# A mixture-of-experts kernel: the last expert's few-slot products in four pieces instead of one run

## The chip, the cores and the metric

The kernel runs on one core of a Trainium2 chip. The metric is device time in microseconds (us) of the whole program, the median of the runs; lower is better. The core has TensorE (PE, matrix products; PEld is its weight load), VectorE (DVE), ScalarE (ACT), GpSimd (POOL, which issues the gathers here) and SyncE (SP, which issues plain transfers). ACT issues some transfers too.

## The reference

Three layers follow each other. Only the last two matter here:

```
# layer 2: each token goes to one expert e (8 of them), x is 2 x 768 tokens of 512
h = np.maximum(x[b, s] @ w1[e], 0.0)
out[b, s] = p[e] * (h @ w2[e])
# layer 3, on that output x
theta = x @ w_theta
zr, zi = x * np.cos(theta), x * np.sin(theta)
y = np.einsum('ts,bsd->btd', w_tok_r, zr) + np.einsum('ts,bsd->btd', w_tok_i, zi)
u = x + y
result = u + np.maximum(u @ w_ch, 0.0)
```

Layer 1 is a local attention that makes the x of layer 2.

## The kernel before, in words

Tokens are sorted by expert into slots. The eight experts are taken in the order of their loads, each with a fixed capacity of slots (288 down to 144), in tiles of 128. The last expert, with 144, has a full tile and a rest of 16 slots ("few", held 32 wide). Results by slot are written to a buffer in HBM, yd, and layer 3 gathers its rows back in token order, in 12 blocks of 128 tokens (k = 0 to 11).

The few slots of the last expert are handled by a Python generator, `y_few`: it takes a PSUM tile `few`, issues the products of `mm2_few` (L1596: 32 matrix products, eight for each of four pairs of hidden chunks, weights 32 columns wide and 128 columns streamed), then scales the sum on ACT into the tile y0 (L1656, shown in rows as y<-few) and stores it from SP to yd (L1657). Each `next(few)` in layer 3's code issues what stands up to the next `yield`.

Layer 3 works block by block. For block k, in the program's names:

- `gather_y(k)` (L1774) and `gather_q(k)` (L1783, four quarter gathers) bring rows of yd to SBUF, as yg and xq.
- `h_tr(k)` transposes the block: blocks 0 and 1 on PE (L1807, sixteen products with the identity, b<-yg), later ones on DVE (L1798, xTf<-xq).
- `h_xh(k)` (L1814, ACT) and `h_xl(k)` (L1827, DVE) split the result into a high part xh and a low part xl.
- `h_theta(k)` (L1843, PE) makes theta in 12 products: eight with xh, four with xl.
- `trig_a`, `trig_s`, `trig_b`, `trig_c` turn theta into the parts z of x·sin and x·cos, on ACT and DVE (sine at L1871, high parts z at L1904 on ACT, low parts at L1909 on DVE). Blocks 0 and 1 do this in two halves of 256 columns, `lo` and `hi`.
- `h_mix(k, d)` (L1929, PE) multiplies z by the token weights, for a quarter d of the columns, in 12 products. d = 0 and 1 use the half `lo`, d = 2 and 3 the half `hi`.

The text calls these theta(k), mix (k, d), xh(k) and so on. Each engine works through its own list in the order in which the code above issues it (the order is written by hand; no scheduler changes it), and waits by semaphores for other engines' results. `job_load` issues loads of layer-3 weights, here from ACT's queue; `JBUFS` is 3. At the start of layer 3 the order by hand is: theta(0), transposes of block 0, few, transposes of block 1, trig(0) `lo`, mix (0,0), theta(1), trig(0) `hi`, mix (0,1), and on.

Of the kernel before, what the change touches and what calls it, by code (L numbers as in the profile page):

```python
# [104 lines left out]
def by_quad(ap):  # L105

    return ap.rearrange("p (q j c) -> p j q c", q=4, c=32)
# [8 lines left out]
def kernel(  # L116
# [1270 lines left out]
    with ExitStack() as mctx:  # L1387
# [9 lines left out]
        def width(r, i):  # L1397


            M = RCAP[r] - i * 128  # L1400
            return 32 if M <= 32 else 64 if M <= 64 else 128
# [186 lines left out]
        def mm2_few(u, out=None):  # L1588

            r = u // 8  # L1590
            i = RTILES[r] - 1
            c, out = width(r, i), out or yps[r][i]
            for v in (u, u + 1):
                hx, w = fews.pop(v)
                for g in range(128 // c if c < 128 else 0):
                    PE.matmul(  # L1596
                        out[g * c : (g + 1) * c, : 4 * c],
                        lhsT=hx[:, :c],
                        rhs=w.rearrange("p (j q c) -> p q j c", q=4, c=32)[:, g * c // 32 : (g + 1) * c // 32],
                        start=(v % 8 == 0),  # L1600
                        stop=(v % 8 == 7),
                    )
# [15 lines left out]
        def groups_out(n, M, W):  # L1618

            return yd[n : n + M, :].rearrange("m (g c) -> g m c", c=W)  # L1620
# [26 lines left out]
        def y_few():  # L1647

            out = pA_[0].tile([128, 512], F32, tag="a", name="few")
            yield  # L1650
            for u in range(8 * E - 8, 8 * E, 2):
                mm2_few(u, out)
            yield
            W, M = 4 * width(E - 1, 1), width(E - 1, 1)
            yo = y0[:, 384 : 384 + W]
            A.activation(yo, out[:, :W], AF.Copy, scale=pslot.pop(RBASE[E - 1] + 1))  # L1656
            SP.dma_start(groups_out(YLAST + 128, M, W), yo)  # L1657
# [107 lines left out]
    with ExitStack() as hctx:  # L1765
# [24 lines left out]
        def h_tr(k, pool=None):  # L1790
            if k >= NB:
                return
            b, t = divmod(k, NT)
            if t == 0:
                xTb[b] = hb.tile([128, 4, S], F32, tag="xTf", name="xTf")
            if k >= VT:
                xps[k] = xTb[b][:, :, t * 128 : (t + 1) * 128]
                V.transpose(  # L1798
                    xps[k].rearrange("p j (i a) -> p i j a", i=4),
                    xqs.pop(k).rearrange("p (i j c) -> p i j c", i=4, j=4),  # L1800
                )
                return
            tp = (pool or pB).tile([128, 4, 128], F32, tag="a" if pool else "b", name="b")
            for j in range(4):
                for q in range(4):
                    rows = by_quad(x2s[k])[:, j, q]
                    PE.matmul(tp[32 * q : 32 * q + 32, j], lhsT=rows, rhs=ident, start=True, stop=True)  # L1807
            xps[k] = tp
# [26 lines left out]
        def h_theta(k, pool=None):  # L1835
            if k >= NB:
                return
            xh, xl = xparts.pop(k)
            th = ths[k] = (pool or pB).tile([128, DM], F32, tag="a" if pool else "b", name="th")
            prods = ((xh, wth[0]), (xh, wth[1]), (xl, wth[0]))  # L1840
            for n in range(12):
                (xa, wa), j = prods[n // 4], n % 4
                PE.matmul(th, lhsT=xa[:, j], rhs=wa[:, j], start=(n == 0), stop=(n == 11))  # L1843

        def trig_a(k, c=slice(0, DM), tick=lambda: None):

            if k >= NB:
                return
            if k not in trig:
                trig[k] = [hb.tile([128, DM], F32, tag=n, name=n, bufs=2) for n in ("kk", "rr", "si")]  # L1850
            th = (ths[k] if k else ths[k][c.start // 256])[:, c]
            kk, rr, si = [x[:, c] for x in trig[k]]
            A.activation(kk, th, AF.Copy, scale=1.0 / TWO_PI, bias=MAGIC)
            tick()
            if k < VT:
                V.tensor_scalar(kk, kk, MAGIC, None, op0=ALU.subtract)
            else:
                A.activation(kk, kk, AF.Copy, bias=-MAGIC)
            tick()
            V.scalar_tensor_tensor(rr, kk, -C1, th, op0=ALU.mult, op1=ALU.add)  # L1860
            tick()
            V.scalar_tensor_tensor(rr, kk, -C2, rr, op0=ALU.mult, op1=ALU.add)
            tick()
            V.tensor_scalar(rr, rr, 3.1415925, -3.1415925, op0=ALU.min, op1=ALU.max)

        def trig_s(k, c=slice(0, DM)):

            if k >= NB:
                return
            kk, rr, si = trig[k]  # L1870
            A.activation(si[:, c], rr[:, c], AF.Sin)  # L1871
            A.activation(kk[:, c], rr[:, c], AF.Sin, scale=0.5)
            A.activation(kk[:, c], kk[:, c], AF.Square)
            if k >= VT:

                A.activation(kk[:, c], kk[:, c], AF.Copy, scale=-2.0, bias=1.0)
# [17 lines left out]
        def trig_b(k, c=slice(0, DM), eng=V):  # L1894
            trig_i(k, c, eng)
            trig_r(k, c)
# [20 lines left out]
        def h_mix(k, d):  # L1917
            b, t = divmod(k, NT)
            if t == 0 and d == 0:
                big = [pA.tile([128, 512], F32, tag="a", name="a") for _ in range(6)]  # L1920
                acc[b] = [(big[d], big[4 + d // 2][:, (d % 2) * 256 : (d % 2) * 256 + 256]) for d in range(4)]
            z = zs[k]
            n = 0
            for ri in (1, 0):
                c = ri * NT + t
                zh, zl = z[2 * ri], z[2 * ri + 1]
                for za, wa in ((zh, wtok(0, c)), (zh, wtok(1, c)), (zl, wtok(0, c))):
                    for o, lo, hi in ((0, 0, 512), (1, 512, 768)):
                        PE.matmul(  # L1929
                            acc[b][d][o],  # L1930
                            lhsT=za[:, d * 128 : (d + 1) * 128],
                            rhs=wa[:, lo:hi],
                            start=(t == 0 and n == 0 and (o == 0 or d % 2 == 0)),
                            stop=(t == NT - 1 and n == 5 and (o == 0 or d % 2 == 1)),
                        )
                    n += 1
# [56 lines left out]
        xh, xl = [hb.tile([128, 4, 128], F32R, tag=n, name=n) for n in ("xh", "xl")]  # L1993
        pA_.append(pA)
        few = y_few()
        next(few)
        xTb[0] = hb.tile([128, 4, S], F32, tag="xTf", name="xTf")
# [16 lines left out]
        x2s[0] = x.rearrange("p j c -> p (j c)")  # L2014
        next(few)
        h_tr(1)
        lo, hi = halves
        trig_a(0, lo)
        mid = [None, partial(trig_s, 0, lo), None, None, partial(trig_i, 0, lo, V)]
# [13 lines left out]
        trig_l(0, 0, lo)  # L2033
        h_xl(1)
        h_mix(0, 0)
        next(few, None)
        for _ in range(JBUFS):
            job_load()
        jstate["eng"] = SP
        h_theta(1)  # L2040
        trig_s(0, hi)
        trig_b(0, hi, V)
        trig_c(0, hi, V)
# [133 lines left out]
```

## Time and profile before

| | |
|---|---|
| median of 3 runs | 467.25 us (466.7 to 468.66) |
| the profiled execution, its own time | 466.93 us |
| its span, first to last instruction | 465.0 us |
| PE busy | 457.9 us, 98% of the span |
| DVE, ACT, POOL busy | 344.0, 262.3, 142.9 us |
| mean granted clock of PE | 0.999 |

The profiled execution is one run; its span is what the trace shows, and 1.9 us of its time lie around it. Times in rows are us from the span's start; layer 3 begins near 288 us. Busy shares are means over stages with different limits; which engine bounds a stage is read from who waits for whom there. A row of a timeline merges like instructions that follow each other.

### The profile page before, as it was taken

To read this page: it belongs to the slowest core of one execution; us is meant where nothing else is said; L and a number is where in the kernel's file an instruction comes from. 1 tells how busy PE (TensorE), PEld (TensorE's weight loads), DVE (VectorE), ACT (ScalarE), POOL (GpSimd) and SP (SyncE) were. 2 spreads that over 40 slices of the span, in tenths; PEclk is the share of its full clock that TensorE was granted. 3 is DMA by queue.
4 is the path that set the end of the run, shared out by engine and by line. 5 is a ranking of instruction groups with operands and counts; after the bars stand their busy time and mean duration, and the time that the engine had idled before them with its cause. 6 is when DMAs were issued, how large, how long until landed. Compare 5 with 4: busy or idle time off the path is not lost.

```text
span 465.0 us, 9578 instructions
## 1 busy us (share of the span) xinstructions
PE 457.9 (98%) x3346; PEld 378.7 (81%) x3346; DVE 344.0 (74%) x946; ACT 262.3 (56%) x623; POOL 142.9 (31%) x203
## 2 busy tenths in 40 slices
PE   8999999999999999999999999999999999999996
PEld 4677777788888898888787788888888888888886
DVE  5888889768687697887888776687997897741522
ACT  5988786822456666655755544556765665630300
POOL 8602313204032404040514302654874441000400
PEclk9999999999999999999999999999999999999999
DMA  8978577715957788788999993521253110000022
GB/s 241 367 231 248 184 240 253 252 47 158 356 167 225 265 296 270 257 277 270 318 348 307 305 312 132 165 91 48 79 152 109 43 49 24 0 35 34 28 87 93
DMA packets 61770, 85.60 MB, mean 184 GB/s; under 512 B 6248, under 2 KB 40296, under 8 KB 61720
## 3 DMA queue, kind: packets, MB, share of 16 engines
q1 hardware_dynamic: 52212, 62.06, 40.8%
q0 software_dynamic: 5552, 12.55, 8.8%
q10 hardware_dynamic: 3956, 10.36, 6.6%
q8 instruction: 27, 0.44, 0.4%
q14 instruction: 23, 0.19, 0.1%
HBM read 73.56 MB, written 11.38 MB: 183 GB/s over the span
## 4 chain that ended last, share of the span: by engine, by line
PE 90%; ACT 4%; DVE 3%; issue 1%; DMA 1%; POOL 0%; DVEq 0%
PE a L1929 22%; PE o L1580 15%; PE h L1524 10%; PE h L1505 8%; PE b L1966 7%; PE th L1843 7%; PE s L574 4%; PE x L653 3%; PE o L1596 3%; PE pt L629 3%; ACT pr L606 2%; PE tr L1341 1%; PE y L670 1%; DVE sm L596 1%; ACT ps L638 1%; PE h L783 1%
## 5 line engine op out<-in xcount | busy, mean ns | idle before, releaser
L1929 PE MATMUL a<-wtokr,z 128*128 128x512 f32 x480 | 85.3, 336 | 0.0
L1929 PEld LDWEIGHTS a<-wtokr,z 128*128 128x128 f32 x480 | 74.2, 188 | 10.0
L1580 PE MATMUL o<-w2s,hh 128*128 128x512 f32 x192 | 62.7, 406 | 0.0
L606 ACT ACTIVATE pr<-sm,st 128x256 f32<-128x256 f32 (+1 forms) x96 | 46.0, 483 | 15.3 <-DVE st L596 15.2
L1524 PE MATMUL h<-xT,w1s 128*128 128x288 f32 (+3 forms) x384 | 51.4, 284 | 0.5 <-DVE xT L1347 0.5
L1524 PEld LDWEIGHTS h<-xT,w1s 128*128 128x128 f32 x384 | 48.7, 189 | 3.4 <-issue 0.6
L1783 POOL DMA_INDIRECT xq<-yd,Lall x40 | 42.4, 1059 | 25.2 <-issue 9.8
L1487 DVE TENSOR_TENSOR w2s<-raw,w2s 128x512 fp32r<-128x512 f32 x56 | 38.5, 689 | 8.4 <-ACT w2s L1486 8.4
L596 DVE CUSTOM_DVE_ANT_0 sm<-s,bias 128x256 f32<-128x256 f32 (+1 forms) x96 | 34.0, 395 | 9.2 <-PE s L574 5.1
L1505 PEld LDWEIGHTS h<-xT,raw 128*128 128x128 f32 x256 | 37.0, 190 | 4.4 <-issue 3.9
L1505 PE MATMUL h<-xT,raw 128*128 128x192 f32 (+3 forms) x256 | 40.5, 311 | 0.0
L1580 PE MATMUL o<-w2s,hl 128*128 128x512 f32 x96 | 38.0, 396 | 0.0
L1580 PEld LDWEIGHTS o<-w2s,hh 128*128 128x128 f32 x192 | 32.4, 184 | 5.8 <-DVE w2s L1487 1.0
L1486 ACT ACTIVATE w2s<-raw 128x512 fp32r<-128x512 f32 x56 | 34.8, 626 | 2.9 <-DMA raw<-in_w_dram 1.4
L1635 POOL DMA_DIRECT2D yd<-yo x13 | 8.2, 634 | 79.1 <-ACT yo L1631 72.4
L1974 DVE SCALAR_TENSOR_TENSOR ob<-b,xTf 128x512 f32<-128x512 f32 (+1 forms) x16 | 8.8, 558 | 29.0 <-PE b L1966 25.7
L1370 DVE TENSOR_TENSOR w1s<-raw,w1s 128x512 fp32r<-128x512 f32 x32 | 22.0, 689 | 6.9 <-ACT w1s L1369 6.4
L574 PE MATMUL s<-kall,q 64*128 64x256 f32 (+1 forms) x192 | 26.1, 391 | 0.0
L629 PE MATMUL pt<-ident,pr 128*128 128x128 f32 x176 | 24.6, 278 | 0.2
L653 PE MATMUL x<-ps,vv 128*64 128x128 f32 x352 | 24.5, 279 | 0.0
L428 ACT ACTIVATE wtokr<-jw 128x512 fp32r<-128x512 f32 x15 | 9.5, 633 | 24.6 <-DVE jw L425 24.6
L1843 PE MATMUL th<-wth,xh 128*128 128x512 f32 x88 | 22.4, 396 | 0.0
(294 smaller groups left out, 944.3 us busy)
## 6 DMA issues: line engine op xcount, KB each, us to landing
raw<-in_w_dram SPq DMA_DIRECT2D x60, 512.0 KB, 5.4
vv<-in_pack_dram SPq DMA_DIRECT2D x10, 512.0 KB, 6.5
jraw<-in_w_tokT_dram ACTq DMA_DIRECT2D x10, 512.0 KB, 5.0
w<-in_w_dram SPq DMA_DIRECT2D x16, 256.0 KB, 5.4
kall<-in_pack_dram SPq DMA_DIRECT2D x10, 320.0 KB, 5.3
xd<-xt SPq DMA_DIRECT2D x12, 256.0 KB, 2.3
q<-in_pack_dram SPq DMA_DIRECT2D x11, 256.0 KB, 4.4
jraw<-in_w_tokT_dram ACTq DMA_DIRECT2D x10, 256.0 KB, 4.7
```

Of the source, the lines that this page charges most:

```text
L574: PE.matmul(sp[hh][:, 0:W], lhsT=qs[n][half, j], rhs=kall[half, b, j, t * 160 + 160 - W : t * 160 + 160], start=True, stop=True,)
L596: V.tensor_tensor_reduce(out=sm[:, hh, 0:W], in0=ust[u]["s"][hh], in1=bias[:, 2 * j + hh], scale=-0.125, scalar=BIG, op0=ALU.add, op1=ALU.min,
L606: A.activation(pr[:, hh, 0:W], sm[:, hh, 0:W], AF.Exp, bias=st[:, hh : hh + 1], scale=-1.0, accum_out=sums[n][:, 2 * j + hh : 2 * j + hh + 1],
L629: PE.transpose(pt[:, hh, c], pr[:, hh, c * 128 : (c + 1) * 128], ident)
L653: PE.matmul(xp[64 * hh : 64 * hh + 64, j], lhsT=vv[:, i, h * 64 : (h + 1) * 64], rhs=ps[:, hh, c], start=(c == 0), stop=(c == nch - 1),)
L1487: V.tensor_tensor(l2, bb[:, o], f32(h2), op=ALU.subtract)
L1505: PE.matmul(hp[:, :N], lhsT=pieces[u // 2][1][:, j, o * 128 : (o + 1) * 128], rhs=x[:, j, :N], start=(j == 0), stop=(j == 3),)
L1524: PE.matmul(hp[:, :N], lhsT=wa[:, j], rhs=xa[:, j, :N], start=(k == 0), stop=(k == 11))
L1580: PE.matmul(out[:M], lhsT=ha[:, lo : lo + M], rhs=wa, start=(f == 0 and q == 0), stop=(f == 7 and q == 2),)
L1783: G.indirect_dma_start(xq[:, i * 128 : (i + 1) * 128], None, yd.rearrange("n (q w) -> (n q) w", q=4), bass.IndirectOffsetOnAxis(ap=yq[:, i ...
L1843: PE.matmul(th, lhsT=xa[:, j], rhs=wa[:, j], start=(n == 0), stop=(n == 11))
L1929: PE.matmul(acc[b][d][o], lhsT=za[:, d * 128 : (d + 1) * 128], rhs=wa[:, lo:hi], start=(t == 0 and n == 0 and (o == 0 or d % 2 == 0)), sto ...
```

## The change

`y_few` gives control back after each of its four pairs, and the callers ask for one piece at four places: after the transposes of block 0, after those of block 1, after mix (0,0), and after theta(1). The copy and the store come behind the last piece.

```diff
@@ y_few
             for u in range(8 * E - 8, 8 * E, 2):
                 mm2_few(u, out)
-            yield
+                yield
             W, M = 4 * width(E - 1, 1), width(E - 1, 1)
             yo = y0[:, 384 : 384 + W]
             A.activation(yo, out[:, :W], AF.Copy, scale=pslot.pop(RBASE[E - 1] + 1))
@@ start of layer 3
         x2s[0] = x.rearrange("p j c -> p (j c)")
         next(few)
         h_tr(1)
+        next(few)
         lo, hi = halves
         trig_a(0, lo)
@@
         h_xl(1)
         h_mix(0, 0)
-        next(few, None)
+        next(few)
         for _ in range(JBUFS):
             job_load()
         jstate["eng"] = SP
         h_theta(1)
+        next(few)
+        next(few, None)
         trig_s(0, hi)
         trig_b(0, hi, V)
```

On PE, at the start of layer 3, before the change (b is a transposed block, a the sums of a mix, th a theta; wtok and wth are the token and theta weights):

```order
L2013 MATMUL b<-ident,xTf 128x128 x4
L1596 MATMUL few<-late,y_107 32x128 x32
L1807 MATMUL b<-ident,yg 32x128 x16
L1929 MATMUL a<-wtok_95,z_4561 128x512
...
L1929 MATMUL a<-wtok_95,z_4560 128x256
L1843 MATMUL th<-wth_97,xh 128x512 x4
L1843 MATMUL th<-wth_98,xh 128x512 x4
L1843 MATMUL th<-wth_97,xl 128x512 x4
L1929 MATMUL a<-wtok_95,z_4561 128x512
```

The same place on PE after the change:

```order
L2013 MATMUL b<-ident,xTf 128x128 x4
L1596 MATMUL few<-late,y_107 32x128 x8
L1807 MATMUL b<-ident,yg 32x128 x16
L1596 MATMUL few<-late,y_107 32x128 x8
L1929 MATMUL a<-wtok_95,z_4545 128x512
...
L1929 MATMUL a<-wtok_95,z_4544 128x256
L1596 MATMUL few<-late,y_107 32x128 x8
L1843 MATMUL th<-wth_97,xh 128x512 x4
L1843 MATMUL th<-wth_98,xh 128x512 x4
L1843 MATMUL th<-wth_97,xl 128x512 x4
L1596 MATMUL few<-late,y_107 32x128 x8
L1929 MATMUL a<-wtok_95,z_4545 128x512
```

Eight of the 32 products stay ahead of the transposes of block 1; the others stand behind these, behind the first mix, and behind theta(1).

On ACT, at the copy of the few sums, the difference between the two (xTf is the last step of block 1's copies, jraw are the loads of `job_load`, si is the sine of the half `hi` of block 0):

```order
 L1821 ACTIVATE xTf<-b 128x4x128
-L1656 ACTIVATE y_107<-few,pfew 128x128
 L404 DMA jraw<-in_w_tokT_dram 128x1024
 L404 DMA jraw<-in_w_tokT_dram 128x512 x2
 L404 DMA jraw<-in_w_ch_dram 128x1024
+L1656 ACTIVATE y_107<-few,pfew 128x128
 L1871 ACTIVATE si<-rr 128x256
 L1872 ACTIVATE kk<-rr 128x256
 L1873 ACTIVATE kk<-kk 128x256
```

The copy stands behind the loads now, still right ahead of the sine of the second half. On SP the store keeps its place among SP's transfers, and the lists of DVE and POOL are as they were.

## Rows read from the trace of the kernel before

**Rows 1.** The page: the chain's shares by engine, and PE's clock in 40 slices.
```profile
PEclk9999999999999999999999999999999999999999
PE 90%; ACT 4%; DVE 3%; issue 1%; DMA 1%; POOL 0%; DVEq 0%
```
**Rows 2.** The chain in order of time: start, us, what, number of records.
```profile
293.63 1.88 PE few L1596 x64
...
296.60 2.32 PE a L1929 x12
298.92 2.97 PE th L1843 x12
301.89 4.17 PE a L1929 x24
306.06 2.79 PE th L1843 x12
...
436.08 25.01 PE b L1966 x144
```
**Rows 3.** Timeline, 287 to 310 us: start, us, engine, line, what, [idle before <-releaser].
```profile
291.74 0.95 POOL L1774 DMA_INDIRECT yg<-yd,yidx  x1 [5.12 <-DMA yd<-yo]
...
293.56 1.69 PEld L1596 LDWEIGHTS few<-late,y 128*32 128x32 f32 x64 [0.17 <-issue]
...
295.49 0.84 PEld L1807 LDWEIGHTS b<-ident,yg 128*32 128x32 f32 x32 [0.24 <-issue]
```
**Rows 4.** Line 1774 from 291.5 to 292.2 us: the one gather's time to landing.
```profile
DMA to landing us min/median/max: 3.6/3.6/3.6
```
**Rows 5.** Line 1774 from 288 to 350 us: all its gathers.
```profile
DMA to landing us min/median/max: 3.3/3.6/7.3
```
**Rows 6.** Timeline of ACT.
```profile
297.15 0.41 ACT L1904 ACTIVATE z<-kk 128x256 fp32r<-128x256 f32 x1
...
297.93 0.37 ACT L1656 ACTIVATE y<-few,pfew 128x128 f32<-128x128 f32 x1
...
298.50 0.42 ACT L1871 ACTIVATE si<-rr 128x256 f32<-128x256 f32 x1 [0.20 <-issue]
...
302.03 0.63 ACT L1814 ACTIVATE xh<-xTf 128x512 fp32r<-128x512 f32 x1 [1.11 <-DVE xTf L1798]
...
307.72 0.42 ACT L1904 ACTIVATE z<-si 128x256 fp32r<-128x256 f32 x1 [1.61 <-DVE si L1884]
...
322.02 0.63 ACT L1814 ACTIVATE xh<-xTf 128x512 fp32r<-128x512 f32 x1 [0.23 <-DVE xTf L1798]
```
**Rows 7.** Timeline of DVE.
```profile
295.74 0.42 DVE L1892 TENSOR_TENSOR kk<-kk,b 128x256 f32<-128x256 f32 x1
...
298.08 0.69 DVE L1827 TENSOR_TENSOR xl<-b,xh 128x512 fp32r<-128x512 f32 x1
...
300.38 0.42 DVE L1909 TENSOR_TENSOR z<-si,z 128x256 fp32r<-128x256 f32 x1
...
306.67 0.71 DVE L1798 STREAM_TRANSPOSE xTf<-xq 128x512 f32<-128x512 f32 x1 [0.32 <-DMA xq<-yd,Lall]
...
321.28 0.71 DVE L1798 STREAM_TRANSPOSE xTf<-xq 128x512 f32<-128x512 f32 x1
...
330.12 0.70 DVE L1798 STREAM_TRANSPOSE xTf<-xq 128x512 f32<-128x512 f32 x1
```
**Rows 8.** Timeline of PE.
```profile
305.90 2.02 PE L1843 MATMUL th<-wth,xh 128*128 128x512 f32 x8
...
310.79 2.24 PE L1929 MATMUL a<-wtokr,z 128*128 128x512 f32 x12
...
323.99 2.02 PE L1843 MATMUL th<-wth,xh 128*128 128x512 f32 x8
```
**Rows 9.** Waits of SP's queue, 285 to 330 us: total, times, longest.
```profile
SPq L1657 <- DMA xq<-yd,Lall: 17.2, 2, 17.1
```
**Rows 10.** Busy time of each engine in the last 4 us, then clock and DMA.
```profile
461.00:465.00 4.00, 0.07 (x1) 0.00 (x0) 0.42 (x1) 0.00 (x0) 0.00 (x0) 0.89 0.26 68
```

## The prediction

> **What bounds the kernel now.** The page comes first: TensorE (PE) makes up 90% of the chain that ended last, and its granted clock is full in every slice [rows 1]. Next the chain in order of time: from 293.63 us on one PE group ends where the next begins, through the last layer to its last 144 matmuls [rows 2]. So from here PE holds the bound without a gap, and no later wait takes up a delay: what PE loses in this stretch the kernel loses. The question is what PE waits for near the change, and how far off the other engines' results lie. I read that from the timelines of PE, ScalarE (ACT), VectorE (DVE) and the gathers, and note for each result when it is there and when PE wants it.
>
> Few waits are left to win. Mix (0,0) took 2.32 us where two mixes take 4.17, so 2.08 each: 0.24 over. Theta(1) took 2.97 against 2.79 for theta(2): 0.18 over, and DVE's subtraction xl, which it needs, ended only at 298.77 [rows 2, 7]. Together 0.42 us is all that a better order can win back here.
>
> **The change part by part.** The work stays the same: 32 products in one run of 1.88 us [rows 2], so 0.47 a piece. Nothing is removed. Three pieces, 1.41 us, move behind the sixteen transposes b<-yg; ACT's copy y<-few moves behind the last piece, and with it the store on SP; ACT's four loads now stand ahead of the copy and so are not held by it. I follow the delay in steps.
>
> *Step 1, the transposes stand still.* The gather of yg was issued at 291.74 and landed 3.6 us later, at 295.34; the transposes' first weights went in at 295.49 [rows 3, 4]. The four pieces filled just this time: they ended at 293.63 + 1.88 = 295.51. With one piece ahead, PE is done at 294.10 and stands until 295.49, 1.4 us. The transposes gain nothing, and the three pieces cost their full 1.41 us behind them. The profile puts the short gap at the transposes down to "issue"; with the landing only 0.15 before them I take the gather for the last thing that was missing.
>
> A page of the Trainium skill bears on this wait. "DMA: Bandwidth & Descriptors", section "Anatomy of one DMA — SWDGE (gpsimd) path", gives some 2.0 us fixed plus the bytes over 436 GB/s for such a transfer; my estimate from it for 128 rows of 2 KB is 2.6 us, so a landing at 294.3. By that the standstill would be 0.3 us and the whole sum below about 2.2 us. The trace has 3.6 us for this very gather, and the measurement decides.
>
> *Step 2, PE up to mix (0,1).* The transposes end at 296.60 as before [rows 2]. Piece 1 (0.47), mix (0,0) (2.32; I keep its 0.24, which may be start-up), piece 2 (0.47), theta(1) (2.79: its wait for xl is over by then, 0.18 won) and piece 3 (0.47) bring PE to 303.12, where it was at 301.89: 1.23 us late.
>
> *Step 3, ACT is held.* This is the term that decides. ACT works in program order: z<-kk began at 297.15, when xh had left (xh waited for the transposes), though DVE had its input ready at 296.16 [rows 6, 7]. Before, y<-few found its sums long done and ran at 297.93; the sine si of the second half of block 0 followed at 298.50, 0.20 of the distance being "issue" of a load [rows 6]. Now y<-few stands in the same place of ACT's queue, but its sums end with piece 3, at 303.12. With si 0.37 behind it, si starts at 303.49, 4.99 late; I take 4.9, since the chain's ends are modelled ones. Behind si are queued the rest of z(0) hi, the copy xh(2), all of trig(1), xh(3), trig(2) and xh(4), and DVE waits for each in turn. The whole ACT and DVE chain moves by 4.9 us.
>
> *Step 4, who waits for that on PE.* The result's new time comes first, then PE's.
> - Mix (0,2) wants the low part of si of z(0) hi, from DVE at 300.80 + 4.9 = 305.70 [rows 7]. PE arrives at 303.12 + 2.08 = 305.20 and wants it after four of twelve products, at 305.9. No wait, by a hair.
> - Theta(2) wants xh(2): 302.03 + 0.63 + 4.9 = 307.56 [rows 6]. PE arrives at 305.90 + 1.23 = 307.13 [rows 8]: 0.45 with the hand-over. PE is 1.7 late.
> - At the transpose xT(3) DVE had waited 0.32 us for its gather [rows 7]. That wait goes; ACT and DVE are 4.6 late.
> - Mix (1,0) wants the high part of si for block 1: 307.72 + 0.42 + 4.6 = 312.74 [rows 6]. PE arrives at 310.79 + 1.7 = 312.49 [rows 8]: 0.3. PE is 2.0 late.
> - Theta(4) wants xh(4): 322.02 + 0.63 + 4.6 = 327.25 [rows 6]. PE arrives at 323.99 + 2.0 = 325.99 [rows 8]: 1.3. PE is 3.3 late.
> - From there DVE's rounds take 8.84 us (transposes at 321.28 and 330.12 [rows 7]) and PE's 4.17 twice and 2.79, 11.13 [rows 2]. ACT and DVE catch up 2.3 us a round, and xh(5) is early again. No further wait.
>
> *Step 5, the store.* It costs nothing. With y<-few done at 298.3, SP still waited 17.1 us for gathers that read the same buffer in HBM [rows 6, 9], so the store went at about 315.4. These gathers cover it: y<-few at 303.5 is 12 us early. Only as the ACT and DVE chain is late by 4.6, and with it the gathers that wait for buffers which DVE reads, does the store move, to about 320. The next gathers wait for it, and the transposes that want them are late by the same 4.6. Without that cover it would be some 5 us late and eat into the time between store and transpose (315.4 to 330.12).
>
> *Sum:* 1.23 + 0.45 + 0.3 + 1.3 = 3.3 us. Bounds: if the 0.24 at mix (0,0) goes as well and a piece costs 0.42 (1.69 of weight loads in four [rows 3]), y<-few is 0.4 earlier and theta(4) 2.9 late. If each of the three pieces behind the transposes pays such a start-up of 0.24, y<-few is 0.7 later and the sum 4.0. Nothing below is left while ACT is held. The profiled execution took 466.93 us (span 465.0 and 1.9 around it), 0.3 under the median of three, 467.25. 466.93 + 3.3 is 470.2; with some of that 0.3, **470.3 us**.
>
> **The rivals.**
> *A, not slower: the held ACT is not in PE's way.* The ACT and DVE chain would have slack that I do not see, and xh(4) would be on time. Only step 2 is left, 1.23: 468.2 us, which a measurement of this kernel can't tell from no change (it tells about 0.5%, 2.3 us). PE waits for nothing if xh(4) is late by less than 2.5 us, and the total stays inside 2.3 if it is late by less than 3.6, in place of 4.6. Against it: between y<-few and xh(4) I find one wait for something outside these two engines, the 0.32. Chance 11%.
>
> *B, the gather lands early, or was not what PE waited for.* If it landed 1 us earlier, PE and ACT would be that much earlier from step 2 on, and theta(4) 2.3 late: 469.2. If PE need not wait for it at all, the transposes start at 294.10, 1.4 us earlier, and theta(4) is 1.9 late: 468.8. The gathers of this form took 3.3 to 7.3 us to land [rows 5], so an early one is unlikely. Chance 5%. If the ACT chain has slack besides, the 0.42 of waits is won: 466.5, 3%. The rule of the Trainium skill in step 1 ("DMA: Bandwidth & Descriptors") would put the kernel between these, at 469.1 by my estimate.
>
> *C, worse: a second thing is late, or the clock falls.* Late could be the transposes for theta(5), if the gathers behind the store slip by some 5 us more than the chain. As for the clock, it stayed full through all short waits of PE and fell from 2.4 to 1.2 GHz only after the last matmul (461.1 us), since its mean is 0.89 over the last 4 us [rows 10]. The longest standstill that I expect is 1.4 us. Were the clock at its lower level from 295.5 to the end of piece 3, the 7.6 us of work there would take 7.6 more: 477.8. "TensorE: Matmul & The Clock Gate" of the Trainium skill, section "Why this matters for your kernels", warns of gaps between bursts of matmuls for this reason; no row here shows a short one that costs the clock. 472 to 478 us, chance 8%.
>
> **How the numbers follow.** The forecast, 469.8 to 470.9, has 73%. The range from 468.1 to 471.6 leaves out C, the last 3% of B and a little of A. Slower by over 0.5% are the forecast and C without their low edges, 78%; within 0.5% are A and most of B, 19%; faster 3%.
>
> **What would show it.** In the profile after: PE without work for 1.4 us ahead of b<-yg, which still starts at 295.5; y<-few near 303.1 with ACT idle for some 5 us ahead of it, and si right behind; theta(2), mix (1,0) and theta(4) waiting for ACT, theta(4) longest; the store near 320; later rounds all late by one constant. The prediction is wrong if b<-yg starts near 294.2, if si begins before y<-few, or if theta(4) follows its mix without a gap.

## The result and the profile after

The changed kernel takes 470.18 us (median of 6 runs, 469.9 to 471.52); the kernel before, run beside it, 467.12 (6 runs, 466.7 to 468.67). The ratio is 1.0063, with a 95% interval of 1.0042 to 1.0085: 3.0 us slower, between 2.0 and 4.0. The profiled execution took 470.22 us with a span of 468.4, so 3.3 and 3.4 more than the profiled execution of before.

The page of the changed kernel: PE's clock in 40 slices, and the chain's shares, as in [rows 1].

```profile
PEclk9999999999999999999999999999999999999999
...
PE 81%; ACT 6%; DMA 5%; DVE 5%; issue 2%; POOL 1%; SPq 0%; DVEq 0%; POOLq 0%; ACTq 0%
```

The clock is as before. PE's share of the chain fell from 90% to 81%: PE is no longer the only bound from 293 us on. The chain in order of time shows where it lost it and where it takes over again (start, us, what; compare [rows 2]).

```profile
325.72 0.72 DVE xTf L1798
...
326.46 0.64 ACT xh L1814
...
327.14 3.06 PE th L1843 x12
330.20 8.34 PE a L1929 x48
```

Up to 327.14 us the end goes back through ACT and DVE. From theta(4) on it is PE alone again, one group behind the other. So nearly all of the loss is there by 327 us (3.15 us at theta(4), 3.26 at PE's last work), and the place to look is between the first piece and there. PE's timeline follows (start, us, engine, line, what, count, idle time before and its releaser; the rows count two records for each product of a piece, so x16 is one piece of eight):

```profile
293.45 0.64 PE L1596 MATMUL few<-late,y 128*32 128x128 f32 x16
295.05 1.08 PE L1807 MATMUL b<-ident,yg 128*32 128x128 f32 x32 [0.95 <-DMA yg<-yd,yidx]
295.92 0.65 PE L1596 MATMUL few<-late,y 128*32 128x128 f32 x16
296.50 2.35 PE L1929 MATMUL a<-wtok,z 128*128 128x512 f32 x12
298.78 0.64 PE L1596 MATMUL few<-late,y 128*32 128x128 f32 x16
299.35 2.12 PE L1843 MATMUL th<-wth,xh 128*128 128x512 f32 x8
...
302.33 0.65 PE L1596 MATMUL few<-late,y 128*32 128x128 f32 x16
302.90 4.43 PE L1929 MATMUL a<-wtok,z 128*128 128x512 f32 x24
307.50 2.13 PE L1843 MATMUL th<-wth,xh 128*128 128x512 f32 x8 [0.17 <-ACT xh L1814]
...
312.56 2.35 PE L1929 MATMUL a<-wtokr,z 128*128 128x512 f32 x12
...
327.14 2.13 PE L1843 MATMUL th<-wth,xh 128*128 128x512 f32 x8 [1.10 <-ACT xh L1814]
```

Two starts of the kernel before are needed beside these:

```profile
295.52 1.08 PE L1807 MATMUL b<-ident,yg 128*32 128x128 f32 x32
...
301.73 4.33 PE L1929 MATMUL a<-wtok,z 128*128 128x512 f32 x24
```

After the first piece PE stands still for 0.95 us, and the row itself names the gather of yg. Mix (0,1) starts at 302.90, 1.17 later than before; theta(2) at 307.50, 1.60 later than in [rows 8]; mix (1,0) at 312.56, 1.77 later; theta(4) at 327.14, 3.15 later and behind the longest wait, 1.10 us for ACT's xh. Each delay stands on the one before it, and the last is nearly the kernel's loss.

Two intervals part the loss, and both begin after the gather has landed. From the start of the transposes to mix (0,1), where PE does the pieces, it took 6.21 us before and 7.85 after. From mix (0,1) to theta(4), where it waits for ACT, it took 22.26 before (to 323.99, [rows 8]) and 24.24 after. The ACT timeline shows why xh is late (compare [rows 6]).

```profile
303.04 0.37 ACT L1656 ACTIVATE y<-few,pfew 128x128 f32<-128x128 f32 x1 [5.46 <-PE th L1843]
303.31 0.41 ACT L1871 ACTIVATE si<-rr 128x256 f32<-128x256 f32 x1
...
306.82 0.63 ACT L1814 ACTIVATE xh<-xTf 128x512 fp32r<-128x512 f32 x1 [1.11 <-DVE xTf L1798]
...
326.46 0.63 ACT L1814 ACTIVATE xh<-xTf 128x512 fp32r<-128x512 f32 x1 [0.23 <-DVE xTf L1798]
```

ACT stood for 5.46 us ahead of the copy y<-few, and the sine si, whose input had long been there, came right behind it: at 303.31 in place of 298.50. The releaser named is theta's PE line, but the copy reads the sums of the pieces, and the last piece ended at 302.33 + 0.65 = 302.98, right ahead of 303.04: at such a place the releaser is checked against the instruction's operands. DVE's timeline has the other half (compare [rows 7]).

```profile
303.75 0.42 DVE L1884 TENSOR_TENSOR si<-si,b 128x256 f32<-128x256 f32 x1 [5.44 <-ACT si L1871]
...
306.08 0.70 DVE L1798 STREAM_TRANSPOSE xTf<-xq 128x512 f32<-128x512 f32 x1
...
311.05 0.70 DVE L1798 STREAM_TRANSPOSE xTf<-xq 128x512 f32<-128x512 f32 x1
...
334.55 0.70 DVE L1798 STREAM_TRANSPOSE xTf<-xq 128x512 f32<-128x512 f32 x1
```

DVE stood for the same 5.44 us. Its transpose at 306.08 has no idle time before it, and the 0.32 that the next one waited for a gather before is gone at 311.05. Ahead of 306.08 the chain runs back along gathers of xq and not along this hold, because a gather landed at 306.06. By the order in which POOL issues them, that gather (issued at 302.96) is the last quarter for block 3, and the transpose at 306.08 is block 2's, whose last quarter was issued at 296.72 and landed 5.4 us later, at 302.1. So the gather that the chain names is not one that this transpose reads; experiment 4 below bears that out.

### The profile page after: what moved, and what is told of

Same layout as the page of the kernel before. It is cut to its first block, busy times and chain, and to the rows that moved or that the text cites. A ratio compares the mean times of both kernels' runs of the same rounds, so it can differ in the third digit from the quotient of the medians.

```text
span 468.4 us, 9576 instructions
## 1 busy us (share of the span) xinstructions
PE 458.5 (98%) x3346; PEld 378.2 (81%) x3346; DVE 344.0 (73%) x946; ACT 262.4 (56%) x623; POOL 142.3 (30%) x203
## 4 chain that ended last, share of the span: by engine, by line
PE 81%; ACT 6%; DMA 5%; DVE 5%; issue 2%; POOL 1%; SPq 0%; DVEq 0%; POOLq 0%; ACTq 0%
PE a L1929 17%; PE o L1580 15%; PE h L1524 10%; PE h L1505 8%; PE b L1966 7%; PE th L1843 5%; PE s L574 3%; PE x L653 3%; PE o L1596 3%; PE pt L629 3%; ACT pr L606 2%; DMA xq<-yd,Lall 2%; PE tr L1341 1%; PE y L670 1%; ACT ps L638 1%
```

## The experiments

Three readings were set against each other. The first is the prediction's: ACT's queue is held by the copy, and PE waits for what stands behind it. The second leaves ACT out: PE loses only what it does at another time itself, the standstill and the pieces. The third leaves PE's own part out: the hold of ACT is all of the loss. In experiments 2 and 4 the third lies within 0.2 us of the first, so those runs do not tell these two apart; experiments 1 and 3 do, by 1.2 and 1.4 us. Experiments 1 to 4 ran against 466.92 us for the kernel before (17 runs), 5 to 7 against 466.87 (29 runs). Each ratio is to the kernel before.

**1. The pieces as changed, the copy behind the half block's trigonometry.** Against the changed kernel:

```diff
         next(few)
-        next(few, None)
         trig_s(0, hi)
         trig_b(0, hi, V)
         trig_c(0, hi, V)
+        next(few, None)
         h_mix(0, 1)
```

> The four pieces stand on PE as in the change; only ACT's copy of the few sums (and the store behind it) moves behind the second half of trig(0). Theory 1 (PE's standstill at the transposes costs about 1.2 us, the other 2.0 us come from ACT, which the copy holds): the sine of the second half starts near 297.9 and not near 303.3, theta(4) follows its mix without a gap, and the time is 468.3 us, 1.2 over before. Theory 2 (the pieces cost PE all of it, ACT's hold is beside the way): 470.2 as the change. Theory 3 (the hold is all of it): 467.1 as before.

Measured: 468.5 us (468.26 to 469.28), ratio 1.0041 [1.0026, 1.0056]. Its timeline, PE and ACT:

```profile
295.67 1.08 PE L1807 MATMUL b<-ident,yg 128*32 128x128 f32 x32 [1.43 <-DMA yg<-yd,yidx]
...
298.66 0.42 ACT L1871 ACTIVATE si<-rr 128x256 f32<-128x256 f32 x1 [0.47 <-issue]
...
303.53 4.44 PE L1929 MATMUL a<-wtok,z 128*128 128x512 f32 x24
303.66 0.37 ACT L1656 ACTIVATE y<-few,pfew 128x128 f32<-128x128 f32 x1 [2.59 <-PE few L1596]
303.93 0.62 ACT L1814 ACTIVATE xh<-xTf 128x512 fp32r<-128x512 f32 x1
...
325.89 2.02 PE L1843 MATMUL th<-wth,xh 128*128 128x512 f32 x8
```

The sine is back at 298.66 and theta(4) waits for nothing. It comes 1.25 us earlier than in the changed kernel, though this execution's gather took 3.8 us to land instead of 3.3 and its transposes began 0.62 later; with the transposes at the same time it would be 1.9 earlier. So the hold of ACT is worth 1.9 us by the traces and 1.7 by the two medians; by the two ratios, which were measured against different runs of the kernel before and whose intervals overlap, it is 1.0. Of the readings, 470.2 and 467.1 both lie outside the interval (468.1 to 469.5 us), and the first's 468.3 lies in it. The copy itself is no earlier than in the changed kernel, 303.66 against 303.04, and its 2.59 us of waiting cost nothing here: z(0) hi is out ahead of it, and theta(4) has no wait although xh(2), behind it, came only at 303.93. How late the copy is decides less than what is queued behind it.

**2. Three pieces ahead of the transposes, the last where it was.** Against the changed kernel:

```diff
-        next(few)
+        for _ in range(3):
+            next(few)
         h_tr(1)
-        next(few)
...
         h_mix(0, 0)
-        next(few)
```

> Three pieces stand in one go ahead of the transposes of block 1, the last piece with copy and store behind theta(1). Theory 1: PE's standstill at the transposes shrinks to 0.4 us or less, but the copy still waits until about 302.2, so ACT is held for 4.0 us, xh(4) comes at about 326.4 and theta(4) is 2.4 us late: 469.5 us. Theory 2 (PE's standstill alone): 467.5. Theory 3: the hold is all of it and shortens by a fifth only: 469.7.

Measured: 469.42 us (469.08 to 469.71), ratio 1.0055 [1.004, 1.0069]. Its timeline:

```profile
295.71 1.08 PE L1807 MATMUL b<-ident,yg 128*32 128x128 f32 x32 [0.62 <-DMA yg<-yd,yidx]
...
302.57 4.43 PE L1929 MATMUL a<-wtok,z 128*128 128x512 f32 x24
...
302.70 0.37 ACT L1656 ACTIVATE y<-few,pfew 128x128 f32<-128x128 f32 x1 [4.47 <-PE few L1596]
...
326.74 2.14 PE L1843 MATMUL th<-wth,xh 128*128 128x512 f32 x8 [1.04 <-ACT xh L1814]
```

Two of the three pieces behind the transposes are gone, and the kernel is still 2.6 us slower than before: the copy moved up by only 0.34 us, because theta(1) still stands ahead of its last piece and because the transposes began 0.66 later in this execution, whose gather took 3.8 us to land. The second reading, 467.5, falls.

**3. All 32 products in one run, behind the transposes.** Against the kernel before:

```diff
-        next(few)
         h_tr(1)
+        next(few)
```

> All 32 products stand in one go behind the transposes of block 1 and ahead of mix (0,0), copy and store where they were before the change. Theory 1: PE stands 1.4 to 1.9 us at the transposes, the copy comes at about 298.5 and holds nothing, and the two waits of before at mix (0,0) and theta(1) are gone: 468.5 us, 1.4 over before, and theta(4) follows its mix without a gap. Theory 2: the standstill is longer than in the change, so the time is at or over 470.2. Theory 3: 467.1.

Measured: 467.77 us (467.32 to 470.0), ratio 1.0023 [1.0011, 1.0035], so 0.5 to 1.6 us slower. Its timeline:

```profile
295.83 1.08 PE L1807 MATMUL b<-ident,yg 128*32 128x128 f32 x32 [1.55 <-DMA yg<-yd,yidx]
296.70 1.96 PE L1596 MATMUL few<-late,y 128*32 128x128 f32 x64
...
303.57 4.33 PE L1929 MATMUL a<-wtok,z 128*128 128x512 f32 x24
...
325.84 2.02 PE L1843 MATMUL th<-wth,xh 128*128 128x512 f32 x8
```

This was expected at 468.5 and is 0.7 under that. The forecast was 1.4 over a kernel before of 467.1; the ratio gives 1.1 over, and its interval holds the 1.4. The second reading (470.2 or more) and the third (no change) both fall. With the whole run behind the transposes PE stands 1.55 us for the gather and pays for the products behind it. From the transposes' start to that of mix (0,1) PE took 7.74 us (303.57 − 295.83), against 6.21 before (301.73 − 295.52), so 1.53 more. Why the runs show 1.1 is not settled; the profiled execution took 468.54 us, 0.8 over the median, and the gather was issued at 292.38 in it, 0.6 later than before, which one profile can't weigh.

**4. The last piece and the copy later still, behind mix (0,1).** Against the changed kernel:

```diff
         h_theta(1)
+        h_mix(0, 1)
         next(few)
         next(few, None)
...
         trig_c(0, hi, V)
-        h_mix(0, 1)
```

> As the change, but the last piece and the copy stand behind mix (0,1) and not behind theta(1); the work on PE up to mix (0,2) is the same. The hold of ACT is 2.1 us longer. Theory 1 and theory 3: every result of ACT and DVE up to xh(4) comes 2.1 us later, and so does theta(4): 472.3 us. Theory 2: PE has the same work and the same standstill: 470.2.

Measured: 471.98 us (471.69 to 472.88), ratio 1.0117 [1.01, 1.0134]. Its timeline:

```profile
304.84 0.37 ACT L1656 ACTIVATE y<-few,pfew 128x128 f32<-128x128 f32 x1 [7.55 <-PE few L1596]
...
306.63 2.47 PE L1929 MATMUL a<-wtok,z 128*128 128x512 f32 x12 [1.85 <-ACT z L1904]
...
328.88 2.13 PE L1843 MATMUL th<-wth,xh 128*128 128x512 f32 x8 [1.05 <-ACT xh L1814]
```

The copy is 1.80 us later than in the changed kernel, theta(4) 1.74, and the median 1.8 (2.5 by the two ratios); counted from the transposes' start, 294.77 here, the copy is 2.08 later and theta(4) 2.02. Beyond the room that there is, the hold costs its full length. The chain of this kernel's trace passes no gather of xq between the last piece and theta(4), yet DVE's transpose follows the copy at the same distance: at 307.88, 3.04 us behind it, as in the changed kernel (306.08 − 303.04) and in experiment 2 (305.74 − 302.70). So it was the copy, and not the gather landing at 306.06, that set the transpose in the changed kernel. The second reading, 470.2, falls here too.

**5. Three pieces ahead of the transposes, the last one ahead of theta(1).** As experiment 2, with the last piece one group of products earlier; ACT's order is that of the changed kernel. Against the changed kernel:

```diff
-        next(few)
+        for _ in range(3):
+            next(few)
         h_tr(1)
-        next(few)
...
         h_theta(1)
-        next(few)
         next(few, None)
```

> Three pieces stand ahead of the transposes of block 1, as much of the wait for the gather as they can fill; the last piece stands between mix (0,0) and theta(1), where PE waited 0.18 us for xl before, and the copy follows it. Theory 1: the copy comes at about 299.4, so ACT is held 1.4 us and the chain has room for that; PE gains at most the 0.42 us of waits and pays about 0.2 us for the change of shape around the last piece: 467.0 us, between 0.2 under and 0.4 over before. Theory 2 (each piece taken away from ahead of the transposes costs its full time): 467.4. If ACT's hold costs from the first microsecond on: 468.3.

Measured: 467.33 us (466.81 to 468.41), ratio 1.0015 [1.0006, 1.0024]: 0.7 us slower, 0.3 to 1.1. Its timeline:

```profile
295.32 1.08 PE L1807 MATMUL b<-ident,yg 128*32 128x128 f32 x32 [0.18 <-DMA yg<-yd,yidx]
...
298.65 0.64 PE L1596 MATMUL few<-late,y 128*32 128x128 f32 x16
299.23 2.14 PE L1843 MATMUL th<-wth,xh 128*128 128x512 f32 x8
...
299.37 0.37 ACT L1656 ACTIVATE y<-few,pfew 128x128 f32<-128x128 f32 x1 [1.52 <-PE few L1596]
...
302.14 4.33 PE L1929 MATMUL a<-wtok,z 128*128 128x512 f32 x24
...
324.40 2.02 PE L1843 MATMUL th<-wth,xh 128*128 128x512 f32 x8
```

Against experiment 2 one thing differs: the last piece stands ahead of theta(1) and not behind it. That is worth 0.4 points of ratio, 1.9 us, without a product more or less. PE itself takes the same up to mix (0,1) in both, 6.86 and 6.82 us from the transposes' start; the difference lies behind it, 24.17 and 22.26 us from mix (0,1) to theta(4). The last 0.7 is mostly the one piece, which takes 0.58 us here (299.23 − 298.65) and wins no wait back; 467.0 was expected, a little too low. The second reading's 467.4 fits this run as well as the first, so it does not part these two; that a hold costs from its first microsecond on, 468.3, falls.

**6. A quarter of the products, in the place of before.** Against the kernel before:

```diff
-            for u in range(8 * E - 8, 8 * E, 2):
+            for u in range(8 * E - 8, 8 * E - 6, 2):
...
-                        stop=(v % 8 == 7),
+                        stop=(v % 8 == 7 or v == 8 * E - 7),
```

> The order of before with 24 of the 32 products left out (only the first of the four pairs of hidden chunks is summed for the last expert's few slots), so 1.41 us less work on PE, in one piece. Theory 1 (the products fill a wait for the gather of yg): PE is done at about 294.1 and stands until the gather has landed, and the time is 0.0 to 0.5 us under before, 466.7. If PE's work counts in full there: 1.4 under before, 465.5.

Measured: 466.69 us (465.88 to 467.53), ratio 0.9996 [0.9987, 1.0006]. Its timeline:

```profile
294.63 0.65 PE L1596 MATMUL few<-late,y 128*32 128x128 f32 x16
296.37 1.08 PE L1807 MATMUL b<-ident,yg 128*32 128x128 f32 x32 [1.09 <-DMA yg<-yd,yidx]
```

PE does 1.41 us less, on what the page calls the bounding engine, and nothing is won: it stands 1.09 us for the gather instead. In the kernel before, these products lay in a wait that is there anyway. (The profiled execution, 467.53 us, is the slowest of this kernel's runs, and layer 3 comes later in it.)

**7. The order of before on PE, only the copy and its store later.** Against the kernel before:

```diff
-        next(few, None)
         for _ in range(JBUFS):
             job_load()
...
         trig_c(0, hi, V)
+        next(few, None)
         h_mix(0, 1)
```

> The order of before on PE, with only ACT's copy of the few sums and its store moved behind the second half of trig(0), where nothing waits for them. Theory 1: the copy at its old place cost ACT 0.6 us of a chain that has over a microsecond of room, and the store goes out at its old time, as it waits for gathers: 466.9 us, the same as before. If the place of the copy on ACT matters by itself: 0.5 us or more under before, 466.4 or less.

Measured: 466.64 us (466.19 to 468.64), ratio 1.0002 [0.999, 1.0014]. Its timeline:

```profile
300.40 0.35 ACT L1656 ACTIVATE y<-few,pfew 128x128 f32<-128x128 f32 x1
...
323.56 2.02 PE L1843 MATMUL th<-wth,xh 128*128 128x512 f32 x8
```

The copy runs 2.5 us later than before and the time is the same: its place in the queue costs nothing as long as nothing has to wait for it.

**The two intervals side by side.** They are differences of starts in each kernel's PE timeline, in us; experiment 4 is left out, since its last piece stands inside the second interval.

| | transposes to mix (0,1) | mix (0,1) to theta(4) |
|---|---|---|
| before | 6.21 | 22.26 |
| changed | 7.85 | 24.24 |
| 1, copy behind the trigonometry | 7.86 | 22.36 |
| 2, three pieces ahead, copy held 4.47 | 6.86 | 24.17 |
| 3, one run behind | 7.74 | 22.27 |
| 5, three pieces ahead, copy held 1.52 | 6.82 | 22.26 |
| 6, a quarter of the products | 6.26 | 22.25 |
| 7, order of before, copy late | 6.20 | 22.26 |

The first interval follows the number of products behind the transposes. The second is 22.3 us in every kernel but the two in which the copy held the sine for over 4 us; there it is 1.8 to 2.0 longer. That is the price of the hold in the traces.

## Why the prediction was right, step by step

The forecast was 470.3 us and 470.18 was measured. The mechanism and its order are the trace's; a term of step 1 and one of step 2 were mis-sized, and one row was misread in step 5. That the two terms cancel, and that the total came within 0.2 us, is luck: the gather's time to landing alone differed by 0.5 us between profiles.

*Step 1, the standstill.* Right in kind, and experiments 3 and 6 show it from both sides: take the products away, or put them behind, and PE stands for the gather. The size was too large, 0.95 us in PE's row in place of 1.4: the gather landed 3.3 us after its issue, at 294.93, and the transposes began at 295.05, 0.47 earlier than before. The estimate worked out from the Trainium skill's "DMA: Bandwidth & Descriptors" (section "Anatomy of one DMA — SWDGE (gpsimd) path"), 2.6 us, is under the 3.3 to 3.8 us that this gather took in the changed kernel and experiments 1, 2 and 4.

*Step 2, PE up to mix (0,1).* Forecast 1.23 us late; by starts it is 302.90 against 301.73 in the trace of before, 1.17. The parts were otherwise: from the transposes' start to mix (0,1) PE took 7.85 us in place of 6.21, so three pieces cost 1.64 and not the 1.41 less 0.18 of the sum. A piece holds 0.47 of products but takes 0.57 from its start to the next product's (298.78 to 299.35, 302.33 to 302.90), and the 0.18 that was to be won at theta(1) was not: 299.35 to 302.33 is 2.98 us, 298.83 to 301.73 before was 2.90. PE's own term was thus too small by 0.41, and the standstill too large by 0.47. The forecast's upper bound did allow a start-up, of 0.24 a piece; 0.10 came.

*Step 3, the hold.* The term that decides, and right: y<-few at 303.04 (forecast 303.12), si at 303.31 (303.49), so ACT is 4.81 us late (4.9). Experiment 1 takes the hold away alone, 2 keeps it with fewer pieces behind, 4 lengthens it; the time follows each time.

*Step 4, who waits.* Mix (0,2) had no wait, as forecast by a hair; experiment 4, with 1.80 us more, shows a wait there, 1.85 us, for ACT's high part. Theta(2) was 1.60 late (1.7), DVE's 0.32 at the transpose was absorbed, mix (1,0) was 1.77 late (2.0) and so added 0.17 and not 0.3, theta(4) 3.15 (3.3), and after it no further wait. PE's last work ended 3.26 us later than before.

*Step 5, the store.* Right in what moves it, wrong in the row. The queue of SP has the store at 319.81 us (forecast: about 320; before, 315.36). SP's waits for it in the changed kernel (us in total, times, longest), and the one of before that [rows 9] does not have:

```profile
SPq L1657 <- DMA xq<-yd,Lall: 16.7, 1, 16.7
SPq L1657 <- DMA yg<-yd,yidx: 13.5, 1, 13.5
```

```profile
SPq L1657 <- DMA yg<-yd,yidx: 8.6, 1, 8.6
```

The 17.1 us of [rows 9] do not follow the copy: SP's wait for xq was over by about 306.4, where the first semaphore record of the store's line stands, and the wait that held the store until 315.36 is the next one, 8.6 us for a gather of yg that was issued at 311.91. That 298.3 and 17.1 add up to 315.4 is a coincidence. In the changed kernel that gather was issued at 316.29, 4.38 later, so the store moved with the late chain, as forecast, and the 5 us by which the copy was late were covered.

DVE's transpose for theta(5) followed at 334.55, 4.43 late, and theta(5) still came without a gap.

*The rivals.* A, that ACT's hold is not in PE's way, falls with experiment 2 and with the second interval. B, an early gather, came true by 0.3 us in the profiled execution and was used up by the dearer pieces. Of C neither part came: no second result was late, and the clock stayed full through the standstill and the waits. The stretch of the standstill in the view of busy time by windows (length, busy time of PE, PEld, DVE, ACT and POOL with counts, granted clock, DMA share, GB/s):

```profile
294.00:295.00 1.00, 0.10 (x4) 0.00 (x0) 0.97 (x3) 0.85 (x3) 0.87 (x1) 1.00 0.56 184
```

PE works for 0.10 of 1.00 us, and the clock is 1.00, the upper of its two levels. "TensorE: Matmul & The Clock Gate" of the Trainium skill (section "Why this matters for your kernels") warns of gaps between bursts of matmuls for the clock's sake; it does not say that so short a one costs it, and here it did not.

What stays open: no order tried here is faster than before. The one that keeps the pieces and comes nearest is experiment 5, 0.7 us slower.

## What to carry to other kernels

Before an evacuation is moved behind later products, read what stands behind it in its engine's queue: here a copy of 0.37 us, waiting 5.46 us for the last piece, held the sine behind it and cost about 2 of the 3.0 us by the traces (by the ratios, 1.0 from experiment 1 and 1.9 from 2 and 5). Work that fills a wait is free only there: 1.41 us of products cost nothing ahead of the transposes (taking them away won nothing), and 1.64 in three pieces behind them. To price a hold, carry each late result forward to its reader and subtract the room, wait by wait; past the room it costs its full length.

## What the runs showed of the hardware

Two sizes were not in the sum. A short group of products between groups of another shape takes more than its own share of one run: 0.57 us in place of 0.47. The weight loads of the changed kernel suggest where it goes (timeline, PEld):

```profile
298.78 0.38 PEld L1596 LDWEIGHTS few<-late,y 128*32 128x32 f32 x16 [0.24 <-issue]
299.35 1.69 PEld L1843 LDWEIGHTS th<-wth,xh 128*128 128x128 f32 x8 [0.20 <-issue]
```

The loads of a piece take 0.38 us, and there is idle time of 0.24 ahead of them and 0.20 behind, which the profile puts down to "issue": in the changed kernel's rows a change between 32 and 128 columns of weights shows 0.17 to 0.36 us of it, and the piece right behind the transposes, whose weights are 32 wide too, shows none ahead of it. One run of four pieces has such a change once on either side. That this idle time is what makes a piece dearer is argued from these rows; no run tests it by itself. And one and the same gather landed 3.3 to 3.8 us after its issue from one kernel's profile to the next, which moves PE's standstill with it: single profiles of this stretch are to be compared by intervals from the transposes' start, and kernels by their medians.
